# Logs taken a unit later, and one more pair of transposing DMAs, in a gated linear attention with a GeGLU layer

## The chip, the cores and the metric

The kernel runs on one core of a Trainium2 chip. The metric is the device time of one execution in microseconds (us). One core has five engines that run side by side, each through its own instructions in order: TensorE (PE in the profile; PEld is its weight load), VectorE (DVE), ScalarE (ACT), GpSimd (POOL) and SyncE (SP), which here only issues DMAs. Medians are over three to eleven executions. An execution is called slow when it took over 1.5% more than the fastest one of the same kernel; such ones stay out of the ratios.

## The reference, cut to what matters

```python
mag = sqrt(a_re**2 + a_im**2)                    # B=4, H=8, S=768, D=48
scale = minimum(mag, 0.999) / (mag + 1e-6)
# for each t, with a = scale * (a_re + i a_im):
#   state = a * state + k[t] v[t]^T              (complex, 48 x 48 per head)
#   y[t]  = q[t] @ real(state)
x = y as 3072 tokens x 384
g, val = x @ w_gate, x @ w_val                   # 384 x 1536 each
ffn = (gelu(g) * val) @ w_out                    # 1536 x 384
out = x + sigmoid(x @ w_res) * ffn
```

The kernel cuts the 3072 tokens into 12 groups of 256. Group 0 is unit 0; groups 1 and 2 are unit 1, 3 and 4 unit 2, 5 and 6 unit 3, and so on. For a group it takes the log of |a|^2 and the angle of a, sums both along time on TensorE (`csl`, `cst`), turns these into factors by Exp and Sin, multiplies q and k by them (`padQ`, `padK`), and forms the scores of attention (`at`), which are masked on VectorE (`atm`) and multiplied with v. The attention output x of a unit then goes through the GeGLU layer.

## The kernel before

Each unit passes through two stages. In `phase_x(u)` ScalarE runs Ln, Exp, Arctan and Sin for the groups of unit u+1, while the rest of unit u's attention is done. In `phase_y(u)` it runs the gelus of unit u, and the attention of the next unit begins. Each stage begins with a table load of ScalarE, so the table loads mark the stages in the trace.

The parts that the change touches:

```python
TURN = 3        # groups from TURN on: q and k are turned by DMA, else by TensorE
...
def p1_steps(g):
    def s0():   # the log that is moved, and its scaling by 0.5
        act(out=lm, in_=lm, func=AF.Ln)
        nc.vector.tensor_scalar(out=lm, in0=lm, scalar1=0.5, scalar2=LNMAX, ...)
    ...         # s1, s2: Ln and Exp of a_re, for the angle
def cs_l(g, c): # cumulative sum of lm on TensorE: csl; then Exp to E and Ei on ScalarE
def decay0(g):  # small Exp of row 0 of lm, written over a_re's tile, then stored by DMA
...
def products(g):            # at the end of it, for Q and then K
    if g >= TURN:
        tt = trp.tile([128, C * H, 128], BF, ...)
        T["turn"] = nc.sync.dma_start_transpose(out=tt, in_=pads[nm, g % 2])
...
def attention(g, c):
    # g >= TURN: scores at once from QT and KT
    # else: 8 transposes on TensorE, 1 copy on ScalarE and 1 on VectorE
    #       for each of the four sets of heads, then the scores
    ...
    return [hi(f) for f in (enter, grp(0), dk, grp(1), yy)]   # hi: ahead in order if g < TURN
...
for u in range(NU + 1):     # the main loop
    ...
    for g in gs(u + 2):
        with paced("turn"): # issued after the last DMA turn so far, if there is one
            load_q(g)       # q and k of group g
```

With TURN = 3 there is no turn yet when q and k of groups 3 and 4 are loaded.

Of the kernel before, what the change touches and what calls it, by code (L numbers as in the profile page):

```python
# [16 lines left out]
def weave(*streams):  # L17

    order = []
    for si, (begin, end, steps) in enumerate(streams):  # L20
        n = len(steps)
        for i, step in enumerate(steps):
            order.append((begin + (end - begin) * (i + 0.5) / n, si, i, step))
    for _, _, _, step in sorted(order, key=lambda e: e[:3]):
        step()
# [3 lines left out]
def kernel(  # L29
# [31 lines left out]
    HELD = UNITS[3][-1]  # L61
    DVSQ = (1, 2, 3, 4)
    MAGIC = 12582912.0
    I2PI = 1.0 / (2.0 * math.pi)
    TURN = 3
    LATE0, LATE1 = 0.6, 1.0
    LNMAX = 0.5 * math.log(0.998001)


# [69 lines left out]
    def act(**kw):  # L139
        return tab(nc.scalar.activation(**kw))  # L140
# [60 lines left out]
    def flat(t):  # L201
        return t.rearrange("p c h d -> p (c h d)")


    def paced(nm):
        return tc.issue_after(T[nm].ins) if nm in T else nullcontext()

    def squares(g):

        def q0():  # L210
            T["lm", g] = pS.tile([128, W], FP, tag="s", name="lm")
            with paced("gelu"):
                nc.scalar.activation(out=T["lm", g], in_=flat(T["ar", g]), func=AF.Square)

        def q1():
            if g < 5:
                if g == 0:
                    T["sq"] = hb.tile([128, 4, 2, DM], FP, tag="h2", name="sq0")
                t = T["sq"][:, g % 4].rearrange("p a m -> p (a m)")
            else:  # L220
                t = pE.tile([128, W], FP, tag="E", name="sq")
            T["sq", g] = t
            if g in DVSQ:
                nc.vector.tensor_tensor(out=t, in0=flat(T["ai", g]), in1=flat(T["ai", g]), op=OP.mult)
            else:
                with paced("gelu"):
                    nc.scalar.activation(out=t, in_=flat(T["ai", g]), func=AF.Square)  # L227

        def q2():
            with paced("gmul"):  # L230
                nc.vector.tensor_tensor(out=T["lm", g], in0=T["lm", g], in1=T["sq", g], op=OP.add)  # L231
        return [q0, q1, q2]

    def p1_steps(g):

        def s0():
            lm = T["lm", g]
            act(out=lm, in_=lm, func=AF.Ln)
            nc.vector.tensor_scalar(out=lm, in0=lm, scalar1=0.5, scalar2=LNMAX, op0=OP.mult, op1=OP.min)  # L239

        def s1():
            ar = flat(T["ar", g])
            T["s", g] = pE.tile([128, W], FP, tag="E" if g == 1 else "Ei", name="ra") if g in (1, 2) else ar
            act(out=T["s", g], in_=ar, func=AF.Ln)

        def s2():
            T["th", g] = flat(T["ai", g])
            act(out=T["s", g], in_=T["s", g], func=AF.Exp, scale=-1.0)
            nc.vector.tensor_tensor(out=T["th", g], in0=T["s", g], in1=T["th", g], op=OP.mult)
        return [s0, s1, s2]  # L250
# [95 lines left out]
    def products(g):  # L346
# [10 lines left out]
        def mk(nm, src):  # L357
            def x():
# [3 lines left out]
                T[nm, g] = t  # L362
                if g >= TURN:
                    tt = trp.tile([128, C * H, 128], BF, tag=nm + "T", name=nm + "T")
# [41 lines left out]
    def attention(g, c):  # L406
# [13 lines left out]
        def grp(hg):  # L420
            def turned():
                x0 = c * H + hg * 4
                st["qk", hg] = T["QT", g][0:DD, x0:x0 + 4]
                at = psA.tile([128, 4, 128], FP, tag="at", name="at")
                for j in range(4):
                    nc.tensor.matmul(out=at[:, j], lhsT=T["KT", g][0:DD, x0 + j], rhs=T["QT", g][0:DD, x0 + j],  # L426
                                     start=True, stop=True)
                atm = sqp.tile([128, 4, 128], BF, tag="atm", name="atm")
                nc.vector.tensor_tensor(out=atm, in0=at, in1=mask4, op=OP.mult)  # L429
                st["atm", hg] = atm  # L430

            def a():
                if g >= TURN:
                    turned()
# [53 lines left out]
        def hi(f):  # L488
            if g >= TURN:
                return f  # L490
# [134 lines left out]
    def call(f, *a):  # L625
        return lambda: f(*a)

    def zip_steps(lists):
        return [st[i] for i in range(max(map(len, lists), default=0)) for st in lists if i < len(st)]
# [14 lines left out]
    def phase_x(u):  # L644

        pend = []
        g1 = gs(u + 1)
        p1g = [g for w in range(NU) if P1AT.get(w, w - 2) == u for g in gs(w)]
        now = [g for g in p1g if g in g1]
        ahead = [g for g in p1g if g not in g1]  # L650
        ops = [call(op_step, u - 1, jj) for jj in range(len(gs(u - 1)) * C)]
        att = att_steps(u, 1)
        if not g1:
            weave((0.0, 0.8, att), (0.1, 1.0, ops))
            return

        def csl(g, c):
            pend.append(cs_l(g, c))

        def ex():  # L660
            pend.pop(0)()

        def p1(g):
            return (squares(g) if g == HELD else []) + p1_steps(g) + [call(decay0, g)]
        csls = [call(csl, g, c) for g in g1 for c in range(C)]
        exs = [ex for _ in g1 for _ in range(C)]
        dec = [call(decay2, g) for g in g1]
        cst = [call(cs_t, g, c) for g in g1 for c in range(C)]
        sin = [call(p2_sin, g) for g in g1]
        table("natural_log_exp_and_others")()  # L670
        if now:
            atn = [table("trig_and_small")] + [call(p1_arctan, g) for g in now + ahead]
            pn = zip_steps([p1(g) for g in now])
            weave((0.0, 0.05, pn[:2]), (0.06, 0.1, csls), (0.12, 0.25, pn[2:]), (0.26, 0.4, exs),
                  (0.28, 0.48, zip_steps([p1(g) for g in ahead])),
                  (0.5, 0.5, dec), (0.55, 0.65, atn), (0.62, 0.8, cst), (0.9, 0.95, sin),
                  (0.0, 0.8, att), (0.0, 0.25, ops) if u == 1 else (0.1, 1.0, ops))
            return
        atn = [table("trig_and_small")] + [call(p1_arctan, g) for g in ahead]
        weave((0.0, 0.12, csls), (0.05, 0.5, zip_steps([p1(g) for g in ahead])), (0.12, 0.45, exs),  # L680
              (0.46, 0.46, dec), (0.2, 0.65, cst), (0.7, 0.95, atn + sin), (0.0, 0.8, att), (0.1, 1.0, ops))

    def ramp():

        g0, g1, g2 = gs(0) + gs(1)
        pend = {}

        def csl(g):
            pend[g] = [cs_l(g, c) for c in range(C)]

        def ex(g):
            for f in pend[g]:
                f()
            decay2(g)

        def cst(g):
            for c in range(C):
                cs_t(g, c)
        g3, g4 = gs(2)
        p = {g: p1_steps(g) for g in range(5)}  # L700
        q = {g: squares(g) for g in range(5)}
        pr = products(g0)

        def run(*fs):
            for f in fs:
                f()
        table("natural_log_exp_and_others")()
        run(*q[g0], p[g0][0], p[g0][1])
        csl(g0)
        run(p[g1][1], p[g0][2], q[g1][1], p[g1][2])  # L710
        ex(g0)
        run(p[g2][1], q[g2][1], p[g2][2])
        table("trig_and_small")()
        pr[0]()
        pr[2]()
        for g in (g0, g1, g2):
            if g > g0:
                T["f", g] = flat(T["ar", g])
            p1_arctan(g)
            cst(g)  # L720
            if g == g0:
                run(q[g1][0], q[g1][2], q[g2][0], q[g2][2])
        p2_sin(g0)
        pr[1]()
        pr[3]()
        a0 = attention_first(g0, 0, 0)
        table("natural_log_exp_and_others")()
        run(p[g1][0], p[g2][0])
        run(*a0[:2])
        csl(g1)  # L730
        csl(g2)
        run(*a0[2:4], *q[g3], p[g3][1], p[g3][2])
        ex(g1)
        run(*a0[4:7], *q[g4], p[g4][1])
        ex(g2)
        run(p[g4][2], p[g3][0], p[g4][0], call(decay0, g4), *a0[7:])
        with tc.issue_after(T["row"].ins):
            load_q(2, T["ld", "w", 2])
        table("trig_and_small")()
        p2_sin(g1)  # L740
        p2_sin(g2)
        with tc.issue_after(T["ld", "k", 2].ins):
            load_a(5)
        load_w_out()
        with tc.issue_after(T["ld", "ai", 5].ins):
            load_a(6)
        p1_arctan(g3)
        p1_arctan(g4)
# [75 lines left out]
```

## Time and profile before

| | before |
|---|---|
| median of 3 executions | 293.25 us (292.29 to 293.33) |
| span of the profiled execution | 293.4 us, mean granted TensorE clock 0.957 |
| TensorE, VectorE, ScalarE busy | 84%, 75%, 68% |

The profiled execution took 295.23 us, 0.7% above the median; its positions are used only to a few tenths of a us.

The fifth is VectorE's first use of q of group 3. The second half of q was issued at 63.29 us and took 4.8 us to land, so these data had been there since about 68.1 us:

```profile
77.90 0.95 DVE L349 TENSOR_TENSOR q<-q,E 128x768 bf16<-128x768 f32 x1
```

### The profile page before, as it was taken

To read this page: it belongs to the slowest core of one execution; us is meant where nothing else is said; L and a number is where in the kernel's file an instruction comes from. 1 tells how busy PE (TensorE), PEld (TensorE's weight loads), DVE (VectorE), ACT (ScalarE), POOL (GpSimd) and SP (SyncE) were. 2 spreads that over 40 slices of the span, in tenths; PEclk is the share of its full clock that TensorE was granted. 3 is DMA by queue.
4 is the path that set the end of the run, shared out by engine and by line. 5 is a ranking of instruction groups with operands and counts; after the bars stand their busy time and mean duration, and the time that the engine had idled before them with its cause. 6 is when DMAs were issued, how large, how long until landed. Compare 5 with 4: busy or idle time off the path is not lost.

```text
span 293.4 us, 5142 instructions
## 1 busy us (share of the span) xinstructions
PE 247.2 (84%) x1848; PEld 148.1 (50%) x1848; DVE 221.0 (75%) x388; ACT 199.7 (68%) x333; POOL 96.0 (33%) x141
## 2 busy tenths in 40 slices
PE   0334956889875899989799999989999998999994
PEld 0122545777432456654366654556545665456782
DVE  0669986698997777979577999787987777564453
ACT  3886799679886669966659984779375655455250
POOL 4022942130436123467305564124911223100220
PEclk9999595799997999999989999999999999999999
DMA  8999999999999999979999959999499565910631
GB/s 146 187 174 188 138 201 187 179 165 203 179 168 206 155 177 183 169 153 143 193 203 175 106 109 173 212 179 99 58 223 211 100 54 110 193 29 4 160 54 54
DMA packets 176001, 44.01 MB, mean 150 GB/s; under 512 B 165092, under 2 KB 175976, under 8 KB 175976
## 3 DMA queue, kind: packets, MB, share of 16 engines
q1 hardware_dynamic: 140744, 33.05, 67.9%
q0 software_dynamic: 35232, 10.64, 35.6%
q8 instruction: 14, 0.23, 0.4%
q14 instruction: 11, 0.09, 0.1%
HBM read 31.33 MB, written 9.08 MB: 138 GB/s over the span
## 4 chain that ended last, share of the span: by engine, by line
PE 55%; ACT 15%; DVE 13%; DMA 9%; issue 4%; SPq 2%; DVEq 0%; ACTq 0%
PE gp L575 12%; PE vp L579 12%; PE op L599 11%; DMA KT<-padK 6%; ACT L613 3%; PE cst L286 3%; PE csl L267 3%; PE rp L591 3%; PE at L426 2%; ACT ar L140 2%; DVE lm L290 2%; PE dk L468 1%; DMA ai<-in_a_im_dram 1%; DVE lm L291 1%; ACT E L140 1%
## 5 line engine op out<-in xcount | busy, mean ns | idle before, releaser
L140 ACT ACTIVATE h<-gp 128x512 bf16<-128x512 f32 (+1 forms) x84 | 44.6, 536 | 43.4 <-PE gp L575 42.9
L582 DVE SCALAR_TENSOR_TENSOR h<-h,vp 128x512 bf16<-128x512 bf16 (+1 forms) x84 | 50.4, 607 | 23.9 <-PE vp L579 16.0
L575 PE MATMUL gp<-xT,wg 128*128 128x512 bf16 (+1 forms) x252 | 63.7, 362 | 2.1 <-ACT h L140 1.4
L579 PE MATMUL vp<-xT,wv 128*128 128x512 bf16 (+1 forms) x252 | 63.7, 360 | 0.3 <-ACT xT L564 0.2
L599 PE MATMUL op<-wo,h 128*128 128x384 bf16 x288 | 50.9, 326 | 1.4 <-ACT xT L564 0.8
L608 POOL DMA_DIRECT2D out_dram<-x x22 | 20.7, 974 | 53.0 <-DMA out_dram<-ot 49.1
L579 PEld LDWEIGHTS <-wv 128*128 128x128 bf16 x252 | 25.2, 101 | 23.3 <-issue 1.9
L599 PEld LDWEIGHTS <-h 128*128 128x128 bf16 x288 | 27.3, 98 | 18.8 <-issue 2.7
L311 POOL DMA_DIRECT2D m<-d x32 | 23.4, 761 | 37.2 <-DMA d<-ar 19.0
L575 PEld LDWEIGHTS <-wg 128*128 128x128 bf16 x252 | 24.4, 101 | 20.8 <-issue 4.4
L174 POOL DMA_DIRECT2D v<-in_v_dram x24 | 23.0, 965 | 17.2 <-DMA ai<-in_a_im_dram 11.8
L429 DVE TENSOR_TENSOR atm<-at,mask 128x512 bf16<-128x512 f32 x36 | 24.6, 682 | 4.3 <-PE at L426 4.3
L613 ACT ACT_TABLE_LOAD x21 | 26.9, 1283 | 1.1 <-PEq L808 0.7
L197 POOL COPY landed<-k 1x1 f32<-1x1 f32 x9 | 3.7, 408 | 58.7 <-DMA k<-in_k_dram 58.7
L267 PE MATMUL csl<-lm,lt0a 128*128 128x384 f32 x24 | 12.5, 607 | 10.4 <-DVE lm L239 10.4
L602 DVE SCALAR_TENSOR_TENSOR ot<-sg,op 128x384 f32<-128x384 f32 x24 | 13.1, 548 | 10.7 <-PE op L599 7.2
L286 PE MATMUL cst<-ai,ut0b 128*128 128x384 f32 x40 | 17.4, 523 | 0.3 <-ACT Ei L140 0.3
L140 ACT ACTIVATE CS<-ai,hpi 128x768 bf16<-128x768 f32 x12 | 11.2, 932 | 8.5 <-DVE ai L296 8.5
L426 PE MATMUL at<-QT,KT 96*128 96x128 bf16 x144 | 14.3, 221 | 3.1 <-DMA KT<-padK 2.7
L231 DVE TENSOR_TENSOR lm<-lm,sq 128x768 f32<-128x768 f32 x12 | 11.4, 950 | 7.1 <-ACT sq L227 6.9
L140 ACT ACTIVATE ar<-ar 128x768 f32<-128x768 f32 x20 | 16.8, 851 | 0.0
L481 ACT CAST x<-y 128x384 bf16<-128x384 f32 x22 | 10.5, 478 | 9.0 <-PE y L478 8.6
(112 smaller groups left out, 466.8 us busy)
## 6 DMA issues: line engine op xcount, KB each, us to landing
ar<-in_a_re_dram SPq DMA_DIRECT2D x24, 192.0 KB, 5.6
ai<-in_a_im_dram SPq DMA_DIRECT2D x24, 192.0 KB, 4.7
q<-in_q_dram SPq DMA_DIRECT2D x24, 192.0 KB, 4.8
k<-in_k_dram SPq DMA_DIRECT2D x24, 192.0 KB, 4.9
out_dram<-ot SPq DMA_DIRECT2D x24, 192.0 KB, 2.5
out_dram<-x POOLq DMA_DIRECT2D x22, 192.0 KB, 4.1
v<-in_v_dram POOLq DMA_DIRECT2D x24, 96.0 KB, 4.8
wg<-in_moe_w_gate_dram POOLq DMA_DIRECT2D x4, 288.0 KB, 7.0
```

Source lines behind the costliest of these rows:

```text
L140: return tab(nc.scalar.activation(**kw))
L174: held(nc.gpsimd.dma_start(out=t[:, c], in_=rows(v, g, c)), after)
L267: nc.tensor.matmul(out=cs, lhsT=lmat[c], rhs=T["lm", g][:, sl], start=True, stop=True)
L286: nc.tensor.matmul(out=cs, lhsT=tmat[c if s == 0 else 1], rhs=th[:, sl], start=True, stop=(s == 0 or c == 0))
L311: nc.gpsimd.dma_start(out=m[u * D:(u + 1) * D].rearrange("p r h -> p (r h)"), in_=md.rearrange("r (h d) -> d (r h)", h=H))
L429: nc.vector.tensor_tensor(out=atm, in0=at, in1=mask4, op=OP.mult)
L575: nc.tensor.matmul(out=gp, lhsT=wg[:, fi, ffi * 128:(ffi + 1) * 128], rhs=xT[:, fi, :], start=(fi == 0), stop=(fi == KD - 1))
L579: nc.tensor.matmul(out=vp, lhsT=wv[:, fi, ffi * 128:(ffi + 1) * 128], rhs=xT[:, fi, :], start=(fi == 0), stop=(fi == KD - 1))
L582: T["gmul"] = nc.vector.scalar_tensor_tensor(out=h2[:, ffi, :], in0=h2[:, ffi, :], scalar=0.5, in1=vp, op0=OP.mult, op1=OP.mult)
L599: nc.tensor.matmul(out=ps, lhsT=h2[:, ffi, jj * 128:(jj + 1) * 128], rhs=wo[:, ffi, :], start=(ffi == 0), stop=(ffi == KF - 1))
L608: nc.gpsimd.dma_start(out=out[t0:t0 + 128, :], in_=T["x", token(u, jj)], accum_op=OP.add)
L613: tab(nc.scalar.preload_act_table_set(nm))
```

## The change

It has two parts. The logs of groups 3 to 6, with their scalings and small Exps, are taken one stage later than before (`LAZY`), those of 3 and 4 out of the ramp: less work ahead of the first gelus. And group 2 too is turned by DMA (`TURN = 2`): 32 transposes on TensorE and eight copies on ScalarE and VectorE less around the start of unit 1's stage. In the ramp a few instructions of group 0 also change places.

```diff
-    TURN = 3
+    TURN = 2
+    LAZY = 2
...
         def p1(g):
-            return (squares(g) if g == HELD else []) + p1_steps(g) + [call(decay0, g)]
+            st = p1_steps(g)[1:] if u < LAZY else p1_steps(g) + [call(decay0, g)]
+            return (squares(g) if g == HELD else []) + st
+        lns = [f for g in g1 for f in (p1_steps(g)[0], call(decay0, g))] if u <= LAZY else []
...
-        weave((0.0, 0.12, csls), ...
+        weave((0.0, 0.1, lns), (0.06, 0.16, csls) if lns else (0.0, 0.12, csls), ...
...
-        run(*q[g0], p[g0][0], p[g0][1])
+        run(q[g0][0], p[g0][1], q[g0][1], q[g0][2], p[g0][2], p[g0][0])
         csl(g0)
-        run(p[g1][1], p[g0][2], q[g1][1], p[g1][2])
+        run(p[g1][1], q[g1][1], p[g1][2])
...
-        run(p[g4][2], p[g3][0], p[g4][0], call(decay0, g4), *a0[7:])
+        run(p[g4][2], *a0[7:])
```

More of the change, by code (lines that the diff above doesn't have):

```diff
@@ L679, in phase_x @@
         atn = [table("trig_and_small")] + [call(p1_arctan, g) for g in ahead]
-        weave((0.0, 0.12, csls), (0.05, 0.5, zip_steps([p1(g) for g in ahead])), (0.12, 0.45, exs),
+        weave((0.0, 0.1, lns), (0.06, 0.16, csls) if lns else (0.0, 0.12, csls), (0.05, 0.5, zip_steps([p1(g) for g in ahead])), (0.12, 0.45, exs),
               (0.46, 0.46, dec), (0.2, 0.65, cst), (0.7, 0.95, atn + sin), (0.0, 0.8, att), (0.1, 1.0, ops))
```

## The prediction

> **What bounds the kernel now.** I read first the busy row and the 40 slices of the page, then the chain in order of time, then the table of stretches, and last the SyncE queue alone, because half of the change goes through that queue.
>
> ```profile
> PE 247.2 (84%) x1848; PEld 148.1 (50%) x1848; DVE 221.0 (75%) x388; ACT 199.7 (68%) x333; POOL 96.0 (33%) x141
> ...
> DMA  8999999999999999979999959999499565910631
> ```
>
> TensorE is busy for 84% of 293.4 us, so 46 us are idle. The DMA row is as telling: nine tenths or more from 7 us on to about 125 us. The stretches say where the idle TensorE time lies:
>
> ```profile
> core 0: us, PE busy (x) PEld busy (x) DVE busy (x) ACT busy (x) POOL busy (x), PEclk, DMA share, GB/s
> ...
> 30.00:46.00 16.00, 11.41 (x93) 7.67 (x94) 14.44 (x24) 13.62 (x25) 11.99 (x15) 0.71 1.34 174
> 46.00:70.00 24.00, 21.11 (x223) 17.25 (x223) 18.61 (x38) 18.83 (x34) 3.64 (x6) 0.85 1.27 177
> 70.00:90.00 20.00, 14.77 (x104) 8.28 (x102) 18.00 (x31) 18.33 (x31) 7.30 (x11) 1.00 1.44 182
> 90.00:112.00 22.00, 20.08 (x140) 10.22 (x141) 16.70 (x28) 14.25 (x26) 6.20 (x9) 0.92 1.16 178
> 112.00:134.00 22.00, 20.43 (x148) 12.17 (x147) 18.28 (x32) 19.09 (x30) 12.35 (x19) 1.00 1.19 165
> ```
>
> Until 46 us it is the ramp. From 70 to 90 us, the part before the gelus of unit 1, ScalarE (18.3 of 20) and VectorE (18.0) bind and TensorE waits 5.2 us. From 90 us on TensorE itself is within 2 us of full in each stage. So a gain must come from before 90 us, and must not be lost in a new wait on its way to the end. The chain shows the ramp's Ln and the one place where a transposing DMA binds:
>
> ```profile
> 42.15 0.95 DVE lm L239 x2
> 44.07 1.28 ACT L613
> ...
> 93.23 9.27 DMA KT<-padK
> ...
> 134.88 9.51 DMA KT<-padK
> ```
>
> The SyncE queue in order of time:
>
> ```profile
> 59.20 3.17 SPq L160 DMA_DIRECT2D ai<-in_a_im_dram  x2
> 62.41 3.87 SPq L168 DMA_DIRECT2D q<-in_q_dram  x2
> 66.32 5.97 SPq L168 DMA_DIRECT2D k<-in_k_dram  x2
> ...
> 87.96 0.40 SPq L330 DMA_DIRECT2D d<-E  x1
> 88.46 1.25 SPq L606 DMA_DIRECT2D out_dram<-ot  x2
> 89.83 3.29 SPq L365 DMA_TRANSPOSE QT<-padQ  x1
> 93.23 3.87 SPq L365 DMA_TRANSPOSE KT<-padK  x1
> ```
>
> It issues with no gap from 45 to 103 us, so anything put into it pushes all behind it.
>
> **What the Trainium skill says.** (1) Perfetto Trace Analysis, "What 'DMA-bound' means": an issuing engine whose track is solid DMA slices is itself a bound. The trace agrees for SyncE from 45 to 103 us. (2) DMA: Bandwidth & Descriptors, "Issuing engines are not separate DMA queues": all issuers share 16 DMA engines, so the weight and v loads of GpSimd slow SyncE's. The trace fits: a load pair is issued in about 2.0 us at 12 to 16 us, but takes 3.87 and 5.97 us for q and k of group 3 while the three wo loads run. (3) ScalarE: Activation LUTs, "What ACT_TABLE_LOAD costs": 186 ns + 0.833 ns a column, back-to-back instructions overlapping by some 93 ns. For 768 columns that is 826 ns; the trace has 827 to 887 for the Ln and steps of 0.74 us, so I count 0.74 us for each Ln removed. (4) VectorE: DVE Perf Modes, "The three transpose paths": a 128x128 turn is 390 ns on TensorE and 1309 by DMA. The trace differs in context: four TensorE turns take 0.38 us together, and 16 blocks in one DMA are issued in some 3.5 us and land 5.9 to 6.4 us after issue. The trace's durations are used.
>
> **Part by part.**
>
> (a) Start of the ramp. ScalarE waits 1.24 us for ai of group 0 and 1.02 us for the VectorE sum. Ln(ar) and Exp of group 0 (0.74 us each, now at 9.69 and 11.16) move into these gaps. But the first Exp of the cumulative sums needs lm, the 0.5-scaling and TensorE: that tile is ready at about 12.1 us and read at 12.63. So of 1.5 us about **-0.5 us** is real.
>
> (b) Ramp, two Ln (40.41) and one small Exp for the first decay (43.12): 2 x 0.74 + 0.45 = 1.9 us of ScalarE and two 0.5 us scalings on VectorE. These scalings stand in the chain (0.95 us) ahead of the masks of group 0's attention, and the table load of 44.07 waits behind the small Exp. All is on the path to the first gelu at 52.5 us: some -2 us. Against it stand the loads of group 5: the Square of ai runs at 62.66 us and these data landed at 61.2 (GpSimd's wo load had waited for them), so not much over 1.5 us can be kept: **-1.5 us**.
>
> (c) Unit 1's stage before its gelus (70 to 90 us). Ln of groups 3 and 4 come in, of 5 and 6 go out: nothing in the sum, though the new ones stand ahead of the cumulative sums. One small Exp less: 0.45 us. Group 2's turns go: four ScalarE copies, of 0.58 us but 0.48 in steps, are 1.9 us; four VectorE copies of 0.41 are 1.5 us; 32 TensorE turns are 3.1 us where TensorE has room. Two of the four ScalarE copies lie before 70 us. Both binding engines lose 1.5 to 2.4 us of some 18: **-2.0 us**.
>
> (d) Unit 2's stage (112 to 132 us) gets the two Ln of groups 5 and 6 and their small Exps on top of those of 7 and 8: 1.5 + 0.9 = 2.4 us on ScalarE, which has 19.1 of 22 us busy. 2.3 us of its idle time is one wait before the last Sin, so part hides: **+1.3 us**.
>
> (e) Two more transposing DMAs at about 62 us, 2 x 3.5 = 7 us of SyncE's queue. The loads behind them are now also held behind the turn. q and k of group 3 landed by 76.4 us and k of 4 by 80.1, whereas their products end at 92 us, so this slack takes up most of 7 us. The turns of groups 3 and 4 stand behind those loads: their wait cost TensorE 0.8 us and would grow by up to 5. I charge **+1.0 us**, as a mean over a hidden delay and a visible one.
>
> Sum: -0.5 - 1.5 - 2.0 + 1.3 + 1.0 = -1.7, so 293.25 - 1.7 = 291.55. Because the scheduler may place the freed gaps better than I can by hand, I round down to **291.0 us**.
>
> **Rivals.** *First: the SyncE queue becomes the bound.* For it: no gap from 45 to 103 us, and KT in the chain twice with over 9 us. The turn of group 3 would be issued at about 95 instead of 89.8, its K land at 108 instead of 102.5 while the gelus start earlier. Further, ar of groups 5 and 6 is kept until the late small Exp has left it by DMA, and the loads of groups 9 and 10 that refill these four buffers stand ahead of outputs in the queue (113 us). That would put +5 to +8 us in place of (e): 296 to 299 us. Against it: the a-loads (76.9 to 87.9) are wanted only at 100.7, and the total of bytes is moved by no more than 7 us of one queue. *Second: group 2's K turn lands too late for its attention.* Now padK is done at 64.8 and the first turns run at 65.4; by DMA, K would land about 10 us later, 72 to 75 us. If TensorE's order has these products ahead of the cumulative sums, it stalls there up to 5 us, and (c) is cancelled: 293 to 295 us. Against it: x of group 2 is not needed for the gelus until 90. *Third: all is on the path.* If (b) and (c) count in full, at -2.4 each, and (d), (e) hide: 293.25 - 0.5 - 4.8 = 288 us, and with a better fit of the loads 286.
>
> **Range and chances.** The third gives the low end, 285.5; the first, in part, the high end, 297.5. Two per cent are 5.9 us, below 287.4 or above 299.1. Faster by over 2% needs each gain in full and no wait, 0.17. Slower needs the full queue rival and more, 0.13. Within 2%: 0.70.
>
> **What would show it.** Right: the first gelu at about 50.5 instead of 52.5 us; the table load ahead of unit 1's gelus at 86 instead of 89.6; no copies of group 2's qk; ScalarE busier in unit 2's stage by 2.4 us; the later stages as long as before. Wrong: a wait of TensorE on KT of over 3 us at group 2's or 3's products, SyncE held at the loads of groups 9 or 10 by the small Exp's DMA, a wait for ai of group 5 before its Square, or a unit 2 stage longer by over 2 us.

## More of the kernel before

Besides what the prediction shows, five readings are needed. The first is the line of the page on how much the DMA engines moved:

```profile
DMA packets 176001, 44.01 MB, mean 150 GB/s; under 512 B 165092, under 2 KB 175976, under 8 KB 175976
```

The second is ScalarE's table loads in order of time (start, duration). Those below, of nine between 44 and 156 us, are: gelus of unit 0; the first of unit 1's stage before its gelus; gelus of unit 1; gelus of unit 2.

```profile
51.20 1.28 ACT L613 ACT_TABLE_LOAD   x1
...
69.07 1.28 ACT L613 ACT_TABLE_LOAD   x1
...
89.56 1.28 ACT L613 ACT_TABLE_LOAD   x1
...
131.69 1.28 ACT L613 ACT_TABLE_LOAD   x1
```

The third is TensorE around 68 us: group 2's first scores and the first cumulative sums of groups 3 and 4 follow each other with no wait.

```profile
67.48 0.39 PE L449 MATMUL at<-qk 96*128 96x128 bf16 x4
...
68.36 0.81 PE L267 MATMUL csl<-lm,lt0a 128*128 128x384 f32 x2
```

The fourth is the wo loads among the DMA issues; the last number is the median time from issue to landing.

```profile
wo<-in_moe_w_out_dram POOLq DMA_DIRECT2D x3, 384.0 KB, 7.6
```

## The result, and the profile after

Ratios here and below: the mean time of one kernel's fast executions over that of the other's fast executions of the same rounds, with a 95% interval; so not quite the ratio of the medians.

| | before | after |
|---|---|---|
| median | 292.78 us | 304.78 us |
| lowest, highest (4 executions each) | 292.29, 293.33 | 303.76, 306.6 |
| ratio | | 1.0416 [1.0357, 1.0476] |
| span of the profiled execution | 293.4 us | 304.8 us |

The kernel became slower by 12 us, where a gain of some 2 us had been predicted. ScalarE's table loads after, the same four:

```profile
48.32 1.28 ACT L614 ACT_TABLE_LOAD   x1
...
67.89 1.28 ACT L614 ACT_TABLE_LOAD   x1
...
98.74 1.28 ACT L614 ACT_TABLE_LOAD   x1
...
142.65 1.28 ACT L614 ACT_TABLE_LOAD   x1
```

Their differences give an account, good to a few tenths, of the 11.4 us between the two spans:

| stretch | before | after | difference |
|---|---|---|---|
| start to the gelus of unit 0 | 51.20 | 48.32 | -2.88 |
| gelus of unit 0 | 17.87 | 19.57 | +1.70 |
| unit 1 before its gelus | 20.49 | 30.85 | +10.36 |
| from unit 1's gelus to unit 2's gelus | 42.13 | 43.91 | +1.78 |
| from there to the end | 161.71 | 162.15 | +0.44 |

So the ramp gained more than was predicted, and one stage lost 10.4 us. SyncE's queue says what stands at the start of that stage; here the second number is the time for which the issue held the queue, not the time to landing:

```profile
62.16 4.90 SPq L366 DMA_TRANSPOSE QT<-padQ  x1
67.17 10.23 SPq L366 DMA_TRANSPOSE KT<-padK  x1
77.45 1.20 SPq L169 DMA_DIRECT2D q<-in_q_dram  x2
...
101.25 1.98 SPq L366 DMA_TRANSPOSE QT<-padQ  x1
```

The two new turns held the queue for 15 us, not 7. q of group 3 was issued at 77.45 us instead of 62.41, group 3's own turn at 101.25 instead of 89.83. TensorE waited for the turned K (in brackets the idle time just before, and what ended it):

```profile
79.52 0.61 PE L427 MATMUL at<-QT,KT 96*128 96x128 bf16 x4 [10.75 <-DMA KT<-padK]
79.92 1.59 PE L268 MATMUL csl<-lm,lt0a 128*128 128x384 f32 x2
```

The order has also turned round: the cumulative sums of groups 3 and 4 now stand behind group 2's first scores, and so behind this wait. They also ran at half their pace: a pair took 1.59 us where it took 0.81 before, with a granted clock of 0.66 between 70 and 90 us (1.00 before). VectorE and ScalarE, in that order, wait in the same way:

```profile
70.06 0.56 DVE L240 TENSOR_SCALAR lm<-lm 128x768 f32<-128x768 f32 x1 [0.70 <-ACT lm L141]
80.16 0.69 DVE L430 TENSOR_TENSOR atm<-at,mask 128x512 bf16<-128x512 f32 x1 [9.54 <-PE at L427]
80.77 0.55 DVE L240 TENSOR_SCALAR lm<-lm 128x768 f32<-128x768 f32 x1
```

```profile
81.35 0.52 ACT L141 ACTIVATE ar<-lm 1x384 f32<-1x384 f32 x1 [9.86 <-DVE lm L240]
```

Read them as one chain: the scores wait for K, the mask `atm` waits for the scores, the scaling of the second log stands behind the mask in VectorE's order, and ScalarE's small Exp waits for that scaling. TensorE, VectorE and ScalarE all stand for some 10 us, for one transfer. The Trainium skill, PSUM — Partial Sum Buffer, "Engine vs sequencer instructions", says that the queues of ScalarE and VectorE are strictly first in, first out, and that matmuls start in program order. This trace agrees: the log's scaling had nothing to do with K and still ran 0.6 us after the mask that did.

The DMA side, the page's line and the wo loads again:

```profile
DMA packets 180162, 45.07 MB, mean 148 GB/s; under 512 B 169252, under 2 KB 180136, under 8 KB 180136
...
wo<-in_moe_w_out_dram POOLq DMA_DIRECT2D x3, 384.0 KB, 12.4
```

The two turns add 1.06 MB, and the wo loads, which GpSimd issues at 61.86 us, now take 12.4 us to land instead of 7.6. Between 67 and 72 us, with K's turn and these loads in flight, the DMA engines moved 0.45 MB (91 GB/s); in the same stretch before it was 0.95 MB (191 GB/s).

### The profile page after: what moved, and what is told of

It reads as the page before. It is cut to its first block, busy times and chain, and to the rows that moved or that the text cites. A ratio compares the mean times of both kernels' runs of the same rounds, so it can differ in the third digit from the quotient of the medians.

```text
span 304.8 us, 5058 instructions
## 1 busy us (share of the span) xinstructions
PE 248.2 (81%) x1802; PEld 148.9 (49%) x1816; DVE 219.6 (72%) x384; ACT 197.7 (65%) x329; POOL 96.7 (32%) x141
## 4 chain that ended last, share of the span: by engine, by line
PE 61%; ACT 13%; DMA 12%; DVE 7%; issue 4%; SPq 2%; DVEq 0%; ACTq 0%
PE op L600 14%; PE gp L576 13%; PE vp L580 13%; DMA KT<-padK 7%; PE csl L268 5%; PE cst L287 4%; DMA ar<-in_a_re_dram 3%; ACT L614 3%; PE rp L592 2%; PE at L427 2%; DMA ai<-in_a_im_dram 2%; SPq L366 2%; PE tpx L561 2%; PE cst L289 1%; PE dk L469 1%
## 5 line engine op out<-in xcount | busy, mean ns | idle before, releaser
L580 PE MATMUL vp<-xT,wv 128*128 128x512 bf16 (+1 forms) x251 | 62.7, 357 | 0.5 <-ACT sg L141 0.4
L576 PE MATMUL gp<-xT,wg 128*128 128x512 bf16 (+1 forms) x239 | 61.9, 356 | 1.1 <-issue 0.2
L600 PE MATMUL op<-wo,h 128*128 128x384 bf16 x288 | 52.6, 334 | 0.6 <-ACT Ei L141 0.6
L430 DVE TENSOR_TENSOR atm<-at,mask 128x512 bf16<-128x512 f32 x40 | 27.3, 683 | 17.9 <-PE at L427 17.9
L576 PEld LDWEIGHTS <-wg 128*128 128x128 bf16 x252 | 24.0, 100 | 18.1 <-issue 1.5
L427 PE MATMUL at<-QT,KT 96*128 96x128 bf16 x160 | 16.1, 223 | 14.0 <-DMA KT<-padK 13.0
L268 PE MATMUL csl<-lm,lt0a 128*128 128x384 f32 x24 | 14.0, 676 | 11.7 <-DVE lm L240 11.5
L427 PEld LDWEIGHTS <-KT 96*128 96x128 bf16 x160 | 11.6, 100 | 20.2 <-DMA KT<-padK 13.5
L482 ACT CAST x<-y 128x384 bf16<-128x384 f32 x22 | 10.5, 477 | 10.4 <-PE y L479 8.5
L232 DVE TENSOR_TENSOR lm<-lm,sq 128x768 f32<-128x768 f32 x12 | 11.4, 950 | 7.7 <-ACT sq L228 7.7
```

Of the source, the lines that this page charges most:

```text
L268: nc.tensor.matmul(out=cs, lhsT=lmat[c], rhs=T["lm", g][:, sl], start=True, stop=True)
L427: nc.tensor.matmul(out=at[:, j], lhsT=T["KT", g][0:DD, x0 + j], rhs=T["QT", g][0:DD, x0 + j], start=True, stop=True)
L430: nc.vector.tensor_tensor(out=atm, in0=at, in1=mask4, op=OP.mult)
L576: nc.tensor.matmul(out=gp, lhsT=wg[:, fi, ffi * 128:(ffi + 1) * 128], rhs=xT[:, fi, :], start=(fi == 0), stop=(fi == KD - 1))
L580: nc.tensor.matmul(out=vp, lhsT=wv[:, fi, ffi * 128:(ffi + 1) * 128], rhs=xT[:, fi, :], start=(fi == 0), stop=(fi == KD - 1))
L600: nc.tensor.matmul(out=ps, lhsT=h2[:, ffi, jj * 128:(jj + 1) * 128], rhs=wo[:, ffi, :], start=(ffi == 0), stop=(ffi == KF - 1))
```

## The experiments

Three theories were told apart. **Order**: the new place of the scores, ahead of sums and logs, makes all engines wait. **Queue**: the turns' time on SyncE and the DMA engines delays all that follows, whatever the order. **Contention**: the wo loads, issued in the same microsecond, stretch the turns. All twelve runs gave the right result. The time before was taken anew with each set of runs, on the same chip: medians 292.16 (first to fourth run), 293.01 (fifth to eighth), 293.1 (ninth to eleventh) and 292.07 (twelfth).

### The logs alone

```diff
 (after)
-    TURN = 2
+    TURN = 3
```

> The changed kernel with group 2 turned on TensorE again (threshold back to 3), so only the late logs and the reordered ramp are left. Theory A (the loss is TensorE's wait for group 2's K turn, which stands ahead of the cumulative sums in its order) and theory B (the loss is the SyncE queue, which the two turns push back) both expect no wait on KT at 68 to 80 us and a total of 289 to 293 us. A third theory, D (the late logs or the buffers they hold longer are a part of the loss) expects 295 us or more.

295.02 us (292.6 to 297.26), ratio 1.005 [0.9993, 1.0106]: the same. The ramp is the reordered one here too. The gelu table of unit 0 was loaded at 47.53 us, 3.7 us earlier than before, that of unit 1 at 87.08 (89.56 before), but unit 2's at 134.04, later than before (131.69). ScalarE waits 2.22 us for ai of group 5, which lands when it did; SyncE waits for the late small Exp of groups 5 and 6 to leave the a_re tiles (9.3 us in all, `DMA d<-ar`); and group 3's K arrives late:

```profile
102.82 0.61 PE L427 MATMUL at<-QT,KT 96*128 96x128 bf16 x4 [4.89 <-DMA KT<-padK]
```

So the late logs gain over 3 us in the ramp and lose them again: the stretch from unit 1's gelu table to the next table, with this wait in it, took 26.3 us instead of 22.2. Whether SyncE's queue is the reason is tested below. The late logs alone do not explain the 12 us.

### The turn alone

```diff
 (before)
-    TURN = 3
+    TURN = 2
```

> The kernel before with nothing but group 2's turns done by DMA (threshold 2). Here the cumulative sums of groups 3 and 4 stand ahead of group 2's score products in TensorE's order, as their logs are taken in the ramp. Theory A expects the wait on KT to be there (8 to 11 us on TensorE) but ScalarE to go on with its Exps and logs during it, so a total of 293 to 298 us, clearly under the changed kernel's 304.8. Theory B expects the loss to be that of the queue, the same as in the changed kernel less the gain of the ramp: 303 us or more.

297.26 us, ratio 1.013 [1.0043, 1.0216]. TensorE waits 5.24 us for K of group 2, less than the 8 to 11 us expected:

```profile
75.61 0.61 PE L426 MATMUL at<-QT,KT 96*128 96x128 bf16 x4 [5.24 <-DMA KT<-padK]
```

In this kernel the cumulative sums stand ahead of the scores. 1.3% and 0.5% do not add up to 4.2%: the two parts hurt each other.

### The scores behind the sums

```diff
 (after, group 2 only)
+    T["cslmm"] = ...the csl matmul
+    with tc.issue_after(T["cslmm"].ins):   # around the scores of group 2
-              ... (0.0, 0.8, att), ...
+              ... (0.17, 0.85, att) if u == 1 else (0.0, 0.8, att), ...
```

The last line also moves the rest of group 2's attention back in the order.

> The changed kernel with one order changed: on TensorE the score products of group 2 stand behind the four cumulative sums of groups 3 and 4 instead of ahead of them; the turns stay on DMA. Theory A expects the Exps at about 72 us instead of 82, the gelus of unit 1 at about 90 us instead of 99, a total of 291 to 295 us. Theory B expects ScalarE to go on but the products of groups 3 and 4 to wait for their q and k, which land at 84 and 90 us: gelus not before 95 us, total 298 us or more.

302.39 us, ratio 1.0322 [1.0258, 1.0387]. TensorE's wait for K fell from 10.75 to 4.28 us, but ScalarE's only from 9.86 to 7.34, now behind the mask and VectorE's sum of squares for group 6 (these squares lie in one of the two buffers of `E`, so the Exp to `E` of group 4 waits for that sum):

```profile
80.88 0.49 ACT L141 ACTIVATE E<-csl 128x384 f32<-128x384 f32 x1 [7.34 <-DVE lm L232]
```

Less than 3 of 12 us came back. TensorE's order alone is not the cause, because VectorE still stood.

### The wo loads behind the turn

```diff
 (after)
     def load_w_out():
-        held(..., T["ld", "ai", 5])
+        held(..., T["turn"])
...
-        load_w_out()          # in the ramp
+        if u == 0:            # in the main loop, after phase_y
+            load_w_out()
```

> The changed kernel with the three wo loads (2.4 MB read) held until group 2's K turn has landed, TensorE's order as in the changed kernel. Theory C (the turns are late because they share the DMA engines with wo) expects the K turn to land at 71 to 73 us instead of 79.5 and the wait on it to shrink from 10.8 us to about 3; the total falls by as much, if wo (landing then at about 81) does not bind in its place: 297 to 300 us. If the turns are slow of themselves or wait in the SyncE queue, K lands at 77 us or later, and the total is 304 us or more.

298.69 us, ratio 1.0177 [1.0106, 1.0249]. The profiled execution was a slow one, so only its queue is read. K's turn held the queue for 2 us instead of 10:

```profile
65.95 1.99 SPq L366 DMA_TRANSPOSE KT<-padK  x1
```

So over half of the loss goes away when the wo loads are held. q and k of groups 3 and 4 and the wo loads themselves still come later than before; which of them sets the rest was not tested.

### The small Exp in a row of its own

```diff
 (the logs alone)
-        e = T["s", g][0:1, 0:DM]               # in the a_re tile
+        e = T["row", ORD[g][0]][32:33, :]      # a spare row of another tile
```

> The late logs and the reordered ramp, group 2 turned on TensorE, and the small Exp of each decay written to a row of its own instead of into the first row of ar. Theory D2 (the late logs gain nothing because SyncE's queue stands 9.3 us at the loads that refill ar, until the DMA that reads the small Exp from it is done, so the K turn of group 3 lands late) expects that wait to be gone, the K turn of group 3 to land before 100.5 us and a total of 289 to 291.5 us, under the 295.0 of the same kernel without the row. The rival (the DMA engines are full up to 100 us, so the turn lands at 102 to 103 us whatever the queue waits for) expects 293 us or more.

293.98 us, ratio 1.0023 [0.9977, 1.0069], against 1.005 with the logs alone. SyncE's wait on `d<-ar` is gone and the wait for group 3's K shrinks from 4.89 to 2.08 us. The intervals overlap, so a gain in time is not shown; nor does it beat the kernel before.

### The turns issued but not used

```diff
 (before)
-                if g >= TURN:
+                if g >= TURN - 1:      # also for group 2; its attention still uses TensorE
```

> The kernel before, with the two transposing DMAs of group 2 issued but not used: its scores still come from TensorE's turns. This measures the DMA and queue cost by itself. Theory A (the loss is that the engines wait for the turn) expects at most 1 us: 292 to 293.5. Theory B (the two turns push the loads of q and k and the next turns back by some 7 us, and that sets the end) expects the same loss as with the turn used, 296 us or more. In between would share the loss of 4 to 5 us that the used turn alone showed (297.3).

298.97 us, ratio 1.0202 [1.0148, 1.0256]. This is the cleanest run: no engine needs these two transfers, and still they cost 6 us. (The loads of q and k of groups 3 and 4 are also paced here, as there is now a turn to wait for.) SyncE's queue, and the wait that is left, for q of group 3 on VectorE:

```profile
70.35 6.87 SPq L365 DMA_TRANSPOSE KT<-padK  x1
77.27 1.20 SPq L168 DMA_DIRECT2D q<-in_q_dram  x2
```

```profile
82.03 0.96 DVE L349 TENSOR_TENSOR q<-q,E 128x768 bf16<-128x768 f32 x1 [4.77 <-DMA q<-in_q_dram]
```

The queue theory holds for this half. q of group 3 had some 10 us of slack in the kernel before (68.1 to 77.90 us), which would have hidden 7 us of queue; the two turns held it for 14.5 us.

### The scores behind the angle sums

```diff
 (after, group 2 only)
+    T["cstmm"] = ...the last cst matmul of the unit
+    with tc.issue_after(T["cstmm"].ins):   # around the scores of group 2
-              ... (0.0, 0.8, att), ...
+              ... (0.66, 0.95, att) if u == 1 else (0.0, 0.8, att), ...
```

Here too the rest of group 2's attention moves with its scores.

> The changed kernel with group 2's score products placed on TensorE behind the last phase sum of group 4, so that nothing of the stage but group 2's own attention stands behind the K turn; the turns stay on DMA. Theory A expects the stage before unit 1's gelus to end near 91 us and a total of 293 to 297 us. Theory B expects the products of groups 3 and 4 to wait for q and k (landing at 84 and 90 us), gelus at 95 us or later, a total of 298 us or more.

301.72 us, ratio 1.0315 [1.0262, 1.0368]. No engine waits for K of group 2 now, and the next wait takes its place:

```profile
80.58 0.96 DVE L350 TENSOR_TENSOR q<-q,E 128x768 bf16<-128x768 f32 x1 [5.96 <-DMA q<-in_q_dram]
```

ScalarE waits 9.95 us behind it. What order alone gives back is again 3 us.

### Squares of group 5 held a stage

```diff
 (the logs alone, small Exp in a row of its own)
-    HELD = UNITS[3][-1]    # group 6
+    HELD = UNITS[3]        # groups 5 and 6
```

> As e5_own_row, and the squares of group 5 are taken in unit 1's stage, as those of group 6 are, so that ScalarE does not stand 2.2 us for ai of group 5 among unit 0's gelus. Expected, if the two waits are the reasons for the lost gain of the late logs: no wait for ai at 59 to 62 us, unit 0's gelus 1.5 to 2 us shorter, 287 to 290 us in total. If the loads bind anyway, the time comes back as a longer wait on the K turn of group 3 and the total is that of e5_own_row.

293.78 us, ratio 1.003 [0.9996, 1.0064]. The wait for ai of group 5 is gone, but it was gone already in the profile of the run before (own row), where unit 0's gelus began later. Unit 0's gelus took 18.1 us here and 17.6 there, and the next part up to unit 1's gelu table, which has the squares now, 22.6 and 19.9. A miss: no version of the logs alone beats the kernel before.

### Idle turns behind the loads

```diff
 (before; two unused turns of group 2, placed after the loads of q and k of groups 3 and 4)
+                with tc.issue_after(T["ld", "k", 4].ins):
+                    nc.sync.dma_start_transpose(out=tt, in_=pads[nm, 0])
```

> The kernel before, plus the two unused transposing DMAs of group 2 as in the idle-turn run, but placed in SyncE's queue behind q and k of groups 3 and 4 and ahead of the loads of a of groups 7 and 8. Theory B1 (position in the queue: what cost 6 us was that q of group 3 was issued at 77 instead of 62): q of group 3 is issued at 62 to 63 us again, no engine waits over 2 us for q or k of group 3, the gelu table of unit 1 is loaded at 89 to 91, total 292 to 295, ratio 0.998 to 1.008. Theory B2 (the time for which the two transposes hold the DMA engines, wherever they stand): total stays at 297 to 300, ratio 1.014 to 1.024.

297.63 us, ratio 1.0164 [1.0101, 1.0228]. q of group 3 is in time again (issued at 61.71), unit 1's gelu table at 91.33, about as the position theory said; the total isn't. The queue carries the delay on to group 3's own turn, issued 7.4 us later than before (89.83):

```profile
97.24 2.77 SPq L365 DMA_TRANSPOSE QT<-padQ  x1
```

The stretch from unit 1's gelu table to the next table is 25.7 us here and 22.2 before. So the unused turns cost 5 to 6 us in both places tried; the place changed who waited for them. They held the queue for 7.6 us here and for 14.5 in the first place, and cost nearly the same.

### Loads not paced by group 2's turn

```diff
 (after)
-                    T["turn"] = nc.sync.dma_start_transpose(...)
+                    i = nc.sync.dma_start_transpose(...)
+                    if g > 2:
+                        T["turn"] = i
```

> The kernel after, but the q and k loads of groups 3 and 4 no longer wait to be issued behind group 2's K turn (the pacing to the last turn counts from group 3 on), so that the scheduler sets them between: q of 3, turn of Q, k of 3, turn of K, k of 3, then 4. Theory B1 (late q and k of groups 3 and 4 are what stops VectorE and TensorE): q of 3 lands 8 us or more earlier; but K of group 2 lands 4 to 6 us later still, at 83 to 86, and as its products stand ahead of the sums in TensorE's order, TensorE's wait grows to 14 us or more: 305 to 309, ratio 1.045 to 1.06. If the pacing alone was the fault: 293 to 296. If neither matters beyond the total of the queue: 303 to 306 as after.

301.81 us, ratio 1.0306 [1.0245, 1.0366]: in none of the three ranges that were named. K's turn was issued 5.6 us later than in the changed kernel and was still done 1.2 us earlier, at 76.15:

```profile
61.92 9.53 SPq L366 DMA_TRANSPOSE QT<-padQ  x1
...
72.81 3.34 SPq L366 DMA_TRANSPOSE KT<-padK  x1
```

TensorE's wait grew to 12.07 us only because it began earlier, at 65.5 us. Now it is Q's turn that runs beside the wo loads and holds the queue for 9.53 us. K's comes after them (the last was issued at 61.2 us and took at most 10.2 us to land) and needs 3.34. K's turn left the queue at 75.2 to 77.4 us in all four kernels with late logs and the wo loads in their old place, and at 67 to 68 in the two with these held. Pacing is worth about 3 us (1.0416 against 1.0306, with intervals that touch).

### Both mends together

```diff
 (the changed kernel, with the edits of "the wo loads behind the turn" and "the scores behind the angle sums")
```

> The kernel after with both earlier mends: the wo loads held until group 2's K turn has landed, and group 2's scores behind the cumulative sums of groups 3 and 4. If contention (6 us) and order (3 us) are separate terms, they add: 304.8 - 6 - 3 = 295 to 297, ratio 1.006 to 1.014. If both only shorten one and the same stall, whose rest is the late q of group 3 behind the turn: 298 to 300, as with wo held alone, with a wait for q of group 3 of 2 to 4 us on VectorE.

303.22 us, ratio 1.0336 [1.0238, 1.0433]: worse than either expectation, and than the wo loads held alone (1.0177, with intervals that touch). Now the wo loads are late, and TensorE waits for them:

```profile
77.00 1.46 PE L601 MATMUL op<-wo,h 128*128 128x384 bf16 x4 [3.62 <-DMA wo<-in_moe_w_out_dram]
```

The mends are not terms of a sum. They choose which transfer is last.

### The logs of groups 3 and 4 early again

```diff
 (after)
-    lns = [...] if u <= LAZY else []
+    lns = [...] if u == LAZY else []          # late logs for groups 5 and 6 only
...
-    run(p[g4][2], *a0[7:])
+    run(p[g4][2], p[g3][0], p[g4][0], call(decay0, g4), *a0[7:])
```

> The kernel after, with the logs, their scalings and the small Exp of groups 3 and 4 back in the ramp; only unit 3's logs stay late, and group 2 is still turned by DMA. In this build the four cumulative sums stand ahead of group 2's scores on TensorE, and VectorE's sum of squares ahead of their mask. Theory (the two parts of the change hurt each other: late logs put the sums of groups 3 and 4, and with them ScalarE's Exps, behind the wait for K): ScalarE's wait for lm shrinks from 9.9 us to under 2, the gelu table of unit 1 comes at 87 to 89 as with the turn alone, total 296 to 298.5, ratio 1.010 to 1.020. Rival (the turn and the loads alone set it, whatever the order of the logs; the late logs of unit 3 or the held buffers cost the rest): 301 to 305, ratio 1.028 to 1.042.

296.75 us, ratio 1.0128 [1.0077, 1.0179] (1.016 by the medians). Of 4.2% only 1.3% is left, as with the turn alone, although unit 3's logs are still late. TensorE still waits 5.54 us for K, VectorE 8.41, ScalarE 8.42; unit 1's gelu table, however, came at 93.17, later than the 87 to 89 that was expected (the turn alone has 94.15, so that expectation was wrong for both). ScalarE shows what the earlier logs change:

```profile
70.94 0.47 ACT L141 ACTIVATE E<-csl 128x384 f32<-128x384 f32 x1
...
82.44 0.48 ACT L482 CAST x<-y 128x384 bf16<-128x384 f32 x1 [8.42 <-PE y L477]
...
85.93 1.28 ACT L614 ACT_TABLE_LOAD   x1
```

The wait is still there, but by then ScalarE has the first group's sums turned into factors, and is ready for the next table 3.5 us after the wait. In the changed kernel it still needs 10.0 us (81.35 to 91.38), two short waits of 3.0 us in all among them. Not all of the gain need be order, however: K also came 2.9 us earlier (read at 76.67 instead of 79.52), as its turn held the queue for 5.33 us and not 10.23.

## Why the prediction was wrong

Two by two, the ratios are: neither part 1, late logs 1.005, turn 1.013, both 1.0416, and the turn with only unit 3's logs late 1.0128. The runs show three causes. They overlap and are not terms of a sum.

**The turn itself: step (e), the one that failed.** The prediction charged "+1.0 us, as a mean over a hidden delay and a visible one", on the ground that "this slack takes up most of 7 us". Both sizes were wrong. The turns held SyncE's queue for 15.1 us, not 7. And the slack was read up to the end of the products at 92 us, while VectorE takes q of group 3 at 77.90: some 10 us, enough for 7 and not for 15. Unused, the two turns cost 6 us in one place and 5 in another; used, with the work of (c) saved, 1.3% or 4 us. That (c) was real work can be seen in the busy times: ScalarE's fell from 199.7 to 197.7 us, VectorE's from 221.0 to 219.6. An estimate that the prediction could have made: each turn writes a tile of 128 x 2048 numbers of two bytes, 0.52 MB (1.06 MB were measured for both), and the trace of the kernel before has 178 GB/s on average between 10 and 125 us, so 6.0 us. It read off that the DMA row stands at nine tenths until 125 us, and then priced the turns by the slack of two loads rather than by the capacity they use up. That bytes rather than queue time set the price is an inference. For it: the unused turns cost 6 and 5 us with 14.5 and 7.6 us of queue. Against it: the rate is not fixed, as the next point shows.

**Contention and size.** The turns were taken at 3.5 us of queue each from those at 90 us. At 62 us, beside the wo loads, they took 4.90 and 10.23. Holding these loads back brought K's turn to 1.99 us and the ratio from 1.0416 to 1.0177. In the stretch from 62 to 78 us, the DMA engines moved 152 GB/s in the changed kernel but 191 in the last experiment, which has the same turns and loads; the difference lies mostly between 67 and 72 us (91 against 183). Why is not settled: in the run with the loads not paced, Q's turn beside the wo loads was as slow, at 184 to 204 GB/s.

**The meeting of the two parts, which the prediction did not have.** It summed (b), (c) and (e) as if independent. Late logs put the sums of groups 3 and 4 behind group 2's scores in TensorE's order and the second log's scaling behind their mask on VectorE. So the wait for K, 5 us with the turn alone, became one of 10.75 us with all the Exps still to come. Putting the logs of groups 3 and 4 back took 7 to 8 us away (2.9% by the ratios), the most of all mends (holding the wo loads took 2.4%); an unknown part of this is K's earlier arrival in that run. The rival called *Second* saw K's wait ahead of the sums, named 5 us, and only set it against (c).

The other steps. **(a)**, -0.5: nothing; the first switch of tables came at 17.59 us instead of 17.18, with the first load landing 0.4 us later. **(b)**, -1.5: right in mechanism. 2.9 us were gained at the first gelu table, 1.2 were left when unit 0's gelus ended, and ScalarE did wait for ai of group 5, for 1.54 us, as said. That the first gelu ran at 50.47 us, just as named (50.5), is partly luck: a copy that waits for TensorE now stands between the table load and it. **(d)**, +1.3: 0.7 measured (unit 2's stage before its gelus took 19.92 us before, 20.63 after). The rival *First* was right that the queue binds: the run with idle turns behind the loads shows its delay of group 3's turn, 7.4 us, and the logs alone show its second half, SyncE waiting on the small Exp's DMA. It was given too little weight because it was set against (e) as an alternative, when it holds together with the second.

Of the signs named for being wrong three came: the wait for K, SyncE held by the small Exp's DMA (5.6 us), and the wait for ai of group 5.

Not settled: how the 7 to 8 us of the meeting divide between TensorE's order, VectorE's, K's later arrival and the lower clock after the pause. Moving the scores on TensorE alone gave back 3 us at most, since VectorE's order kept the wait. No run beat the kernel before.

## What to carry to other kernels

Where the DMA engines are full, price an added transfer first at its bytes over the rate that the trace shows, before asking who waits for it: here this gave 6 us for a measured 5 to 6, and moving the transfer changed the one who waits more than the loss. Read slack up to the first use of the data. Two edits that cost little alone can meet in an in-order engine, so ask of each wait that one edit may add what the other edit has put behind it. And test an added transfer by itself, issued and not used: this tells its cost apart from that of waiting for it.

## What the Trainium skill lacked or had wrong

- VectorE: DVE Perf Modes, "The three transpose paths", gives 1309 ns for a 128x128 turn by DMA. Sixteen such blocks in one DMA would be 20.9 us by that, as an estimate; the runs show a median of 5.9 to 6.4 us from issue to landing in the kernel before, and beside the wo loads 15.6 us for Q's and 12.3 us (67.17 to 79.5) for K's turn. The page does not say that the figure depends on what else the DMA engines carry.
- DMA: Bandwidth & Descriptors lacks what a transposing DMA costs when nothing waits for it and the DMA engines are full with other transfers: two of them, unused, took 6 us (ratio 1.0202) of such a kernel.
- No page that was found tells how much longer a transposing DMA holds the queue that issues it when other transfers run: the same turn held it for 1.99 us with the wo loads kept back and for 10.23 us beside them, and the next load of that queue was issued only after that (67.99 and 77.45 us).
